# Loading one weight block in quarters and taking it up in turn: the first K projection of a gated mixer kernel

## The chip, the cores and the metric

The kernel runs on one core of a Trainium2 chip. The metric is device time in microseconds (us) of one execution, measured over several runs; the median counts. One further execution was recorded by the hardware profiler, and all lines shown as profile come from it. The engines are named as the profile does: PE is TensorE, DVE is VectorE, ACT is ScalarE, POOL is GpSimd and SP is SyncE, which here only issues DMAs.

## The reference

Two branches work on one input `x` of 2048 rows and 512 columns (bfloat16) and are mixed by a gate:

```python
x = A_x
g = _sigmoid((x * gate_w).sum(-1, keepdims=True))
a = _A_ref(x, A_wqkv, A_wo)
b = _B_ref(x, B_w1, B_b1, B_w2, B_b2)
return g * a + (1 - g) * b
```

Branch A is attention with 32 heads of 16 columns over a small window: each row looks at itself and at the seven rows that lie 2, 4, ... 14 rows before it. `x @ wqkv` gives Q, K and V; the logits are scaled by 0.25, rows before the start are masked, a softmax over the eight neighbours weights V, and the result goes through `wo`. Branch B is a LayerNorm of `x` over its columns, then a two-layer network across the rows: `w1` (2048 x 1792) with a bias and GELU, then `w2` (1792 x 2048) with a bias.

## The kernel before

**Tiling.** The rows of `x` are 16 tiles of 128 (`x0` to `x15`), and four blocks of 512 rows (`sb` 0 to 3) for the projections. Q, K and V are made transposed: one group is the output for one `dl` (0 to 3, a slice of 128 of the 512 columns) and one block `sb`. It sums over four slices of the input columns, so a group is four matmuls (L688) of 128x512 into one PSUM bank, followed by one evacuation on ScalarE (`evac`, recorded under the helper's line L469). The transposed `x` that they read comes for block 0 from TensorE transposes (`tx0` to `tx3`, L574, copied out by `ext0` to `ext3`) and for blocks 1 to 3 from DMA transposes (`xT1` to `xT3`, L496).

**Stages on TensorE.** Warm-up matmuls (L559), the transposes, and two short groups `lead0` and `lead1` (L605) of branch B; then the projections (48 groups, L688); then `ph2`, the first layer of branch B (L596), with `sum0` (L779), the logit sums of the first half of the rows, between its groups, and `sum1` for the second half; then `ph3`, the second layer (L913), with `wo0` to `wo15` (L922), the last projection of branch A, added to the same banks.

**Work beside it.** VectorE takes the LayerNorm statistics of each tile (`st2` to `st15`, L751) and some short steps from them (`ln_md` to `ln_mean`), the gate's sums (`z0` to `z15`, L732), the products of Q with shifted K (`qk`, L466), their sums (`qa`), the softmax, and the weighted sums of V (`avm`, `ava`, `avb`, `avc`). `qk0_0_512` is the product for the first half of the rows, `dl` 0, columns 512 on; `qk0_0_0` is that for the first 512. ScalarE evacuates the projections (`evq`, `evk`, `evv`), from block 2 on two groups at a time, and does logarithm, exponential and GELU; `ln_log` and `ln_rstd` are the two small steps that turn the variances into factors. GpSimd issues accumulating DMAs (`qd0`, `qd1_0`, `qd1_4`, `avd`) and gathers. SyncE issues the loads in a written order:

```python
ld_x(2, 2)
ld_w("wk01", 1, 0, 2, "wk")
ld_w("wk23", 1, 2, 4, "wk2")
...
ld_w("wq", 0, 0, 4, "wq")
ld_xt(1)
ld_x(4, 4)
ld_xt(2)
ld_x(8, 4)
ld_xt(3)
ld_x(12, 4)
ld_w("wv", 2, 0, 4, "wv")
```

`wk01` and `wk23` (L524, L525) hold the first and the last two of the four input slices of Wk, `x12` the tiles 12 to 15.

**What sets the order.** Every operation is added with a written duration, what it reads and what it writes. A list scheduler in the kernel (`_Sched`, L129 to L234) then fixes the order on each engine when the program is built. It takes at each step the operation that can start first in its own books; among those that can start at the same moment it takes the smallest value of minus the longest path to the end plus three times a written `prio`, so that a `prio` of -4 counts as 12 us of path (L196). The statistics have -4, the short LayerNorm steps -20. In its books a DMA moves 280 GB/s in a queue and lands 2 us after its last byte, and waiting for another engine adds 0.06. TensorE's operations are chained in the order in which they are written (`PE`, L565), except for `sum0` and `sum1`. On the chip each engine runs its list in that order, with semaphore waits.

**The place of the change.** For block 0 the kernel takes three K groups in halves, and then the rest:

```python
kb = [bank_() for _ in range(3)]
...
for tn, dl in ((0, 0), (0, 1), (0, 2), (1, 3), (0, 3)):
    proj(tn, dl, 0)
```

First come the first halves of three K groups, which need `wk01` alone, then their second halves (L702 and L704), each with its evacuation, and then whole groups: Q 0, Q 1, Q 2, K 3, Q 3. The banks for projections are taken in turn from four (4 to 7).

Of the kernel before, what the change touches and what calls it, by code (L numbers as in the profile page):

```python
# [317 lines left out]
def bass_gated_mix__sliding_local_dilated__mixer_token_mlp__prompt_kernel(nc, A_x, A_wqkv, A_wo, B_x, B_w1, B_b1, B_w2, B_b2, gate_w, out, dbg=None):  # L318
    with contextlib.ExitStack() as es:
# [64 lines left out]
        XTUSE = ["w1s3", "w1s4"]  # L384
# [67 lines left out]
        def col(v_, i):  # L452
            return bass.AP(v_.tensor, v_.offset + i, [list(v_.ap[0]), [1, 1]])
# [4 lines left out]
        def sub(ap_, offs, dims):  # L458
            return bass.AP(ap_.tensor, ap_.offset + offs, [list(ap_.ap[0])] + [list(d) for d in dims])
# [8 lines left out]
        def act(o_, i_, f_, **kw):  # L468
            return lambda e: e.activation(out=o_, in_=i_, func=f_, **kw)  # L469
# [21 lines left out]
        def load(name, dst, src, nbytes, writes, transpose=False, queue="sp", issue=0.5, order=True, deps=(), reads=()):  # L491
            ds = sch.dsem(name)

            def fn(e):
                if transpose:
                    return e.dma_start_transpose(dst, src)  # L496
                return e.dma_start(dst, src)  # L497
            op = sch.dma(queue, fn, nbytes, ds, issue=issue, reads=reads, writes=writes, deps=deps,
                         after=([last_ld[0]] if order and last_ld[0] is not None else []), name=name)
            if order:  # L500
                last_ld[0] = op
            return op

        def ld_x(t0, n):
            load("x%d" % t0, X[:, t0:t0 + n, :], xv[:, t0:t0 + n, :], n * 128 * D * 2, ["x%d" % t for t in range(t0, t0 + n)])

        def ld_w(name, tn, d0, d1, res):
            load(name, WQKV[:, d0:d1, tn * D:(tn + 1) * D], wqkv_v[:, d0:d1, tn * D:(tn + 1) * D], (d1 - d0) * 128 * D * 2, [res])
# [12 lines left out]
        ld_x(1, 1)  # L521
        ld_strip(0)
        ld_x(2, 2)
        ld_w("wk01", 1, 0, 2, "wk")  # L524
        ld_w("wk23", 1, 2, 4, "wk2")  # L525
        load("gw", GW1, bass.AP(gate_w.tensor, gate_w.offset, [[D, 1], [1, D]]), 1024, ["gwr"], issue=0.4, queue="act", order=False)
        load("b1", B1R, B_b1.rearrange("(t p) -> t p", p=128), 4096, ["b1r"], issue=0.4, queue="act", order=False)
        load("b2", B2R, B_b2.rearrange("(t p) -> t p", p=128), 4096, ["b2r"], issue=0.4, queue="act", order=False)
# [9 lines left out]
        def ld_w1(j):  # L538
            st = NLEAD if j < 2 else 0
            load("w1_%d" % j, W1S[W1AT[j]][:, st:NST, :], w1v[:, st:NST, 256 * j:256 * j + 256], (NST - st) * 128 * 256 * 2,  # L540
                 ["w1s%d" % W1AT[j]], order=j < 3)
# [23 lines left out]
        def PE(fn, dur, reads, writes, name, prio=0):  # L565
            op = A("pe", fn, dur, reads=reads, writes=writes, after=([chain[0]] if chain[0] is not None else []), name=name, prio=prio)
            chain[0] = op
            return op
# [23 lines left out]
        def f_ph2(ft, bank, s0, s1):  # L592
            def fn(e):
                ins = None
                for st in range(s0, s1):
                    ins = e.matmul(ps[:, bank, :], lhsT=W1S[W1AT[ft // 2]][:, st, 128 * (ft % 2):128 * (ft % 2) + 128], rhs=(LX if st < NLEAD else X)[:, st, :],  # L596
                                   start=(st == 0), stop=(st == NST - 1))
                return ins
            return fn
# [60 lines left out]
        def xt_res(sb):  # L660
            return XT0 if sb == 0 else ["xt%d" % sb]

        def evac(tn, dl, sb, bank):
            h, o = sb // 2, (sb % 2) * 512
            if tn == 0:
                dst = QH[h][:, dl, o:o + 512]
                A("act", act(dst, ps[:, bank, :], AF.Copy, scale=0.25), 0.6, reads=["b%d" % bank], writes=["q%d_%d" % (dl, sb)],
                  name="evq%d_%d" % (dl, sb))
            elif tn == 1:
                dst = KH[h][:, dl, PAD + o:PAD + o + 512]  # L670
                A("act", act(dst, ps[:, bank, :], AF.Copy), 0.6, reads=["b%d" % bank], writes=["k%d_%d" % (dl, sb)],
                  name="evk%d_%d" % (dl, sb))
            else:
                dst = V5[:, dl, PAD + sb * 512:PAD + (sb + 1) * 512]
                A("act", act(dst, ps[:, bank, :], AF.Copy), 0.6, reads=["b%d" % bank], writes=["v%d_%d" % (dl, sb)],
                  name="evv%d_%d" % (dl, sb))
        ring = [0, [4, 5, 6, 7]]

        def bank_():
            b = ring[1][ring[0] % len(ring[1])]  # L680
            ring[0] += 1
            return b

        def f_proj(tn, dl, sb, bank, d0=0, d1=4):
            def fn(e):
                ins = None
                for dt in range(d0, d1):
                    ins = e.matmul(ps[:, bank, :], lhsT=sub(WQKV, dt * 3 * D + tn * D + dl, [(4, 128)]),  # L688
                                   rhs=XT[:, dt, sb * 512:(sb + 1) * 512], start=(dt == 0), stop=(dt == 3))
                return ins  # L690
            return fn

        WR = {0: ["wq"], 1: ["wk", "wk2"], 2: ["wv"]}

        def proj(tn, dl, sb):
            bank = bank_()
            PE(f_proj(tn, dl, sb, bank), 0.87, xt_res(sb) + WR[tn] + XTUSE, ["b%d" % bank], "pj%s%d_%d" % ("qkv"[tn], dl, sb))
            evac(tn, dl, sb, bank)

        kb = [bank_() for _ in range(3)]  # L700
        for dl in range(3):
            PE(f_proj(1, dl, 0, kb[dl], 0, 2), 0.43, xt_res(0) + ["wk"], ["b%d" % kb[dl]], "pjk%d_0h" % dl)  # L702
        for dl in range(3):
            PE(f_proj(1, dl, 0, kb[dl], 2, 4), 0.43, xt_res(0) + WR[1] + XTUSE, ["b%d" % kb[dl]], "pjk%d_0" % dl)  # L704
            evac(1, dl, 0, kb[dl])
        for tn, dl in ((0, 0), (0, 1), (0, 2), (1, 3), (0, 3)):
            proj(tn, dl, 0)
        for dl in range(4):
            proj(1, dl, 1)
            proj(0, dl, 1)  # L710
# [1 line left out]
          reads=["k%d_1" % dl for dl in range(4)], writes=["khalo"], name="khalo")  # L712
        def proj2(tn, dl, sb):
            b0, b1 = bank_(), bank_()
            assert b1 == b0 + 1
            for b_, s_ in ((b0, sb), (b1, sb + 1)):
                PE(f_proj(tn, dl, s_, b_), 0.87, xt_res(s_) + WR[tn] + XTUSE, ["b%d" % b_], "pj%s%d_%d" % ("qkv"[tn], dl, s_))
            h = sb // 2
# [12 lines left out]
        for t in range(NST):  # L731
            A("dve", (lambda t_: lambda e: e.tensor_tensor_reduce(out=JUNK[:, t_ % 4, :], in0=X[:, t_, :], in1=GWB, scale=1.0, scalar=0.0, op0=ALU.mult, op1=ALU.add,  # L732
                                                                  accum_out=col(Z, t_)))(t), 0.61, reads=["x%d" % t, "gwb", "s4"], writes=["z%d" % t, "jk%d" % (t % 4)], after=[e3],
              name="z%d" % t, prio=-4)
        A("pool", lambda e: e.memset(ZN, 0.0), 0.15, writes=["zn"], name="zn0")
        A("dve", lambda e: e.tensor_scalar(out=ZN[:, 0:NST], in0=Z, scalar1=ZMAX, scalar2=-1.0, op0=ALU.min, op1=ALU.mult), 0.12,
          reads=["z%d" % t for t in range(NST)], writes=["zn"], name="zneg", prio=-30)
# [12 lines left out]
        for t in range(NLEAD, NST):  # L750
            A("dve", (lambda t_: lambda e: e.bn_stats(out=ST6[:, t_, :], in_=X[:, t_, :]))(t), 0.6,  # L751
              reads=["x%d" % t], writes=["st%d" % t], after=[e3], name="st%d" % t, prio=-4)
# [7 lines left out]
          reads=["md"], writes=["vv"], name="ln_var", prio=-20)  # L760
# [3 lines left out]
          reads=["ms", "rstd"], writes=["nmr"], name="ln_nmr", prio=-20)  # L764
        for t in range(NLEAD, NST):
            if t >= NST - LNACT:
                A("act", act(X[:, t, :], X[:, t, :], AF.Identity, scale=col(RSTD2, t), bias=col(NMR, t)), 0.7, after=[ev2[0][t - NST - 1]], reads=["rstd", "nmr"], writes=["x%d" % t],
                  name="ln%d" % t)
            else:
                A("dve", (lambda t_: lambda e: e.tensor_scalar(out=X[:, t_, :], in0=X[:, t_, :], scalar1=col(MS, t_), scalar2=col(RSTD2, t_),  # L770
                                                               op0=ALU.subtract, op1=ALU.mult))(t), 0.33,
                  reads=["rstd", "ms", "st%d" % t], writes=["x%d" % t], name="ln%d" % t, prio=-4)
# [14 lines left out]
        for h in range(2):  # L787
# [43 lines left out]
            if h == 0:  # L831
                A("dve", tt(psub(LOG[0], 0, 32, 0, [(UT_, NW), (1, PAD)]), psub(LOG[0], 0, 32, 0, [(UT_, NW), (1, PAD)]), MASK, ALU.add), 0.2,
                  reads=["mask"], writes=["log0"], name="msk")
# [16 lines left out]
            for c in range(4):  # L850
                for dhi in range(4):
# [5 lines left out]
                                   reads=["att%d" % h], writes=["avw%d_%d_%d" % (h, c, dhi)] + al, after=[prev] if prev else [],  # L857
                                   name="av%d_%d_%d" % (h, c, dhi))
# [10 lines left out]
        for u in range(8):  # L869
            h, c = u // 4, u % 4  # L870
            b = 1 if u % 2 == 0 else 0
# [3 lines left out]
              reads=["avw%d_%d_%d" % (h, c, dhi) for dhi in range(4)] + vr + ["vpad"], writes=PR[b], name="avm%d" % u)  # L875
# [15 lines left out]
        for ft in range(NFT):  # L891
            bank = ft if ft < GL else bank_()
            s0 = NLEAD if ft < GL else 0
            for a_, b_ in ((s0, 8), (8, NST)):
                PE(f_ph2(ft, bank, a_, b_), 0.2165 * (b_ - a_), ["%s%d" % ("lx" if t < NLEAD else "x", t) for t in range(a_, b_)] + ["w1s%d" % W1AT[ft // 2]],
                   ["b%d" % bank], "ph2_%d_%d" % (ft, a_))
            A("act", act(UT[:, ft, :], ps[:, bank, :], AF.Gelu_apprx_tanh, bias=col(B1C, ft)), 0.7, after=[xp0] if ft == 3 else [],
              reads=["b%d" % bank, "b1c"], writes=["ut%d" % ft] + (["wq", "wk", "wk2", "wv"] if ft == 0 else []), name="gel%d" % ft)
            if ft in (1, 3):
                ld_w1(5 + ft // 2)  # L900
        for j in range(8):
# [66 lines left out]
        for hf, (c0, c1) in enumerate(CH):  # L968
            bank = lastb[hf]
            n_ = c1 - c0  # L970
            PE(f_wo(L, bank, c0, c1), 0.87 * n_ / D, ["ot%d" % (L // 2), "wo"], ["b%d" % bank], "wo%d_%d" % (L, hf))
            if hf == 0:
                A("act", act(OUTS[:, NOUT, c0:c1], ps[:, bank, 0:n_], AF.Identity, scale=col(OMG, L), bias=col(C2, L)), 0.4,
                  reads=["b%d" % bank, "omg", "c2"], writes=["outl%d" % hf], name="ev%d_%d" % (L, c0))
# [80 lines left out]
```

## Time and profile before

| what | value |
|---|---|
| median of 3 runs | 164.26 us (164.2 to 165.22) |
| profiled execution, own time | 163.65 us |
| its span (first to last instruction) | 162.4 us |
| granted TensorE clock | 1.00 in the stretches looked at |
| busy: PE, DVE, ACT, POOL | 159.1, 150.7, 78.0, 26.7 us |
| PE waits for a load | 0.2 us, once, for a part of `wqkv` |

Busy times are sums over one engine; a busy PE is not a PE at its peak, since matmuls overlap and their ends are modelled. "L688 ... x12" means 12 instructions of line 688. What stands in brackets behind `<-` is what ended the idle time ahead of an instruction. Times are counted from the start of the span.

### The profile page before, as it was taken

The page shows a single profiled execution, that of the slowest core. Times are in us where ns is not written, and L with a number is a line of the kernel's source. Part 1 is how long each engine was busy: PE and PEld are TensorE (multiplying, and loading weights), DVE is VectorE, ACT ScalarE, POOL GpSimd, SP SyncE. Part 2 cuts the span into 40 slices and gives each one's busy share as a digit, 9 for nine tenths or more (in the row PEclk, how much of TensorE's full clock was granted, in tenths as well). Part 3 has the DMA queues.
Part 4 walks back from the last instruction along what each step waited for, and adds up shares of the span by engine and source line. Part 5 has one row for each costly group of instructions (what it writes and reads, how often), then busy time and mean ns, then how long its engine had stood idle before and what let it go on. Part 6 is the DMA issues. An engine that isn't in the chain of part 4 may idle for free.

```text
span 162.4 us, 1994 instructions
## 1 busy us (share of the span) xinstructions
PE 159.1 (98%) x779; PEld 75.9 (47%) x779; DVE 150.7 (93%) x140; ACT 78.0 (48%) x100; POOL 26.7 (16%) x62
## 2 busy tenths in 40 slices
PE   7999999999999999999999999999999999999994
PEld 2445555555554444444444344444444444444652
DVE  2879999999999999999899999999999999999943
ACT  4457665799998281999311345420121111111153
POOL 3000000300000011200792030009580003020000
DMA  5999999999925998999399999999999814949504
GB/s 136 282 218 244 249 312 291 290 262 241 196 63 166 297 290 156 169 292 188 93 292 356 338 295 256 240 322 290 352 215 216 195 39 95 184 110 199 128 32 162
DMA packets 45463, 35.54 MB, mean 219 GB/s; under 512 B 7949, under 2 KB 42254, under 8 KB 45454
## 3 DMA queue, kind: packets, MB, share of 16 engines
q1 hardware_dynamic: 41552, 22.74, 53.3%
q0 software_dynamic: 3696, 12.59, 36.2%
q8 instruction: 6, 0.10, 0.3%
q10 hardware_dynamic: 206, 0.08, 0.2%
q14 instruction: 3, 0.02, 0.0%
HBM read 19.15 MB, written 2.11 MB: 131 GB/s over the span
## 4 chain that ended last, share of the span: by engine, by line
PE 94%; DMA 3%; SPq 1%; DVE 0%; issue 0%
PE ps L913 30%; PE ps L596 29%; PE ps L688 26%; PE ps L922 9%; DMA arena<-in_A_wqkv_dram 3%; PE ps L779 1%; SPq L497 1%; DVE arena L931 0%
## 5 line engine op out<-in xcount | busy, mean ns | idle before, releaser
L466 DVE TENSOR_TENSOR arena<-arena 128x4096 bf16<-128x4096 bf16 (+6 forms) x71 | 125.9, 1806 | 2.7 <-ACT arena L469 1.1
L913 PE MATMUL ps<-arena 128*128 128x512 bf16 (+2 forms) x238 | 50.2, 366 | 0.0
L469 ACT ACTIVATE arena<-ps,arena 128x512 bf16<-128x512 f32 (+1 forms) x29 | 20.9, 727 | 57.1 <-PE ps L922 40.9
L596 PE MATMUL ps<-arena 128*128 128x512 bf16 x216 | 47.1, 379 | 0.0
L688 PE MATMUL ps<-arena 128*128 128x512 bf16 x192 | 41.8, 379 | 0.2 <-DMA arena<-in_A_wqkv_dram 0.2
L469 ACT ACTIVATE arena<-ps 128x512 bf16<-128x512 f32 (+3 forms) x37 | 31.2, 850 | 13.6 <-PE ps L688 9.1
L913 PEld LDWEIGHTS ps<-arena 128*128 128x128 bf16 x238 | 23.3, 98 | 25.4
L596 PEld LDWEIGHTS ps<-arena 128*128 128x128 bf16 x216 | 21.0, 98 | 25.8 <-issue 0.8
L688 PEld LDWEIGHTS ps<-arena 128*128 128x128 bf16 x192 | 21.6, 113 | 20.4 <-DVE arena L650 0.7
L856 POOL DMA_DIRECT2D arena<-arena x32 | 17.0, 660 | 23.1 <-DVE arena L466 14.0
L469 ACT ACTIVATE arena<-arena 128x512 bf16<-128x512 bf16 (+6 forms) x25 | 16.0, 641 | 9.5 <-DVE arena L466 8.9
L922 PE MATMUL ps<-arena 128*128 128x512 bf16 (+2 forms) x68 | 15.6, 366 | 0.0
L807 POOL DMA_DIRECT2D arena<-arena x3 | 3.8, 1270 | 63.0 <-DVE arena L466 35.9
L1004 ACT ACT_TABLE_LOAD x9 | 11.5, 1283 | 2.3 <-issue 2.2
L732 DVE CUSTOM_DVE_ANT_0 arena<-arena 128x512 bf16<-128x512 bf16 x16 | 10.1, 687 | 0.0
L877 POOL DMA_DIRECT2D arena<-arena x4 | 4.9, 1226 | 31.5 <-DVE arena L466 31.5
L922 PEld LDWEIGHTS ps<-arena 128*128 128x128 bf16 x68 | 6.6, 98 | 7.2
L751 DVE BATCH_NORM_STATS2 arena<-arena 128x6 f32<-128x512 bf16 x14 | 8.6, 679 | 0.0
L931 DVE TENSOR_SCALAR arena<-ps,arena 128x512 bf16<-128x512 f32 (+1 forms) x2 | 1.3, 660 | 3.4 <-PE ps L922 3.4
L610 DVE BATCH_NORM_STATS2 arena<-arena 128x6 f32<-128x512 bf16 x2 | 1.4, 678 | 3.0 <-DMA arena<-in_A_x_dram 3.0
L559 PE MATMUL ps<-const-bfloat16-1.0 128*128 128x512 bf16 x6 | 2.9, 580 | 0.8 <-PEq L1040 0.8
L779 PE MATMUL ps<-arena 128*32 128x512 bf16 x32 | 2.1, 382 | 0.0
(38 smaller groups left out, 16.8 us busy)
## 6 DMA issues: line engine op xcount, KB each, us to landing
arena<-in_B_w_dram SPq DMA_DIRECT2D x10, 896.0 KB, 11.6
arena<-arena POOLq DMA_DIRECT2D x6, 1024.0 KB, 9.5
arena<-in_B_w_dram SPq DMA_DIRECT2D x5, 1024.0 KB, 9.4
arena<-arena POOLq DMA_DIRECT2D x32, 128.0 KB, 7.5
arena<-arena POOLq DMA_DIRECT2D x1, 2048.0 KB, 16.3
out_dram<-arena SPq DMA_DIRECT2D x15, 128.0 KB, 1.8
arena<-in_A_x_dram SPq DMA_DIRECT2D x3, 512.0 KB, 4.7
arena<-in_A_wqkv_dram SPq DMA_DIRECT2D x2, 512.0 KB, 6.0
```

The lines of the kernel that those rows point to most:

```text
L466: return lambda e: e.tensor_tensor(out=o_, in0=a_, in1=b_, op=op_)
L469: return lambda e: e.activation(out=o_, in_=i_, func=f_, **kw)
L596: ins = e.matmul(ps[:, bank, :], lhsT=W1S[W1AT[ft // 2]][:, st, 128 * (ft % 2):128 * (ft % 2) + 128], rhs=(LX if st < NLEAD else X)[:, st, :],
L688: ins = e.matmul(ps[:, bank, :], lhsT=sub(WQKV, dt * 3 * D + tn * D + dl, [(4, 128)]), rhs=XT[:, dt, sb * 512:(sb + 1) * 512], start=(dt = ...
L732: A("dve", (lambda t_: lambda e: e.tensor_tensor_reduce(out=JUNK[:, t_ % 4, :], in0=X[:, t_, :], in1=GWB, scale=1.0, scalar=0.0, op0=ALU.m ...
L751: A("dve", (lambda t_: lambda e: e.bn_stats(out=ST6[:, t_, :], in_=X[:, t_, :]))(t), 0.6, reads=["x%d" % t], writes=["st%d" % t], after=[e ...
L807: qdl[0] = sch.dma("pool", (lambda d_, s_: lambda e: e.dma_start(d_, s_, accum_op=ALU.add, max_dma_last_dim=4096))(sub(PB[0], 4096 * b0, r ...
L856: prev = sch.dma("pool", (lambda d_, s_: lambda e: e.dma_start(d_, s_))(dst, src), 131072, ds, issue=1.0, reads=["att%d" % h], writes=["av ...
L877: sch.dma("pool", (lambda d_, s_: lambda e: e.dma_start(d_, s_, accum_op=ALU.add, max_dma_last_dim=4096))(sub(PB[b], 0, [(2048, 2), (1, 20 ...
L913: ins = e.matmul(ps[:, bank, 0:c1 - c0], lhsT=W2S[i // 2][:, ft, 128 * (i % 2):128 * (i % 2) + 128], rhs=UT[:, ft, c0:c1], start=(ft == 0) ...
L922: ins = e.matmul(ps[:, bank, 0:c1 - c0], lhsT=OT[:, i // 2, dl, 128 * (i % 2):128 * (i % 2) + 128], rhs=WO[:, dl, c0:c1], start=False, sto ...
L1004: e.preload_act_table_set(want)
```

## The change

The load of Wk is split into four loads, one for each input slice. For block 0 all four K groups now take a bank each; they take the first slice in turn, then the second in turn, and then each group takes its last two slices and is evacuated. The four Q groups follow. Each of these matmuls is now an operation of its own for the scheduler, with a written duration of 0.217. The names of the four loads take the place of the two wherever they are waited for or their place is written again.

```diff
-        ld_w("wk01", 1, 0, 2, "wk")
-        ld_w("wk23", 1, 2, 4, "wk2")
+        for d_ in range(4):
+            ld_w("wk%d" % d_, 1, d_, d_ + 1, "wk%d" % d_)
...
-        WR = {0: ["wq"], 1: ["wk", "wk2"], 2: ["wv"]}
+        WR = {0: ["wq"], 1: ["wk%d" % d_ for d_ in range(4)], 2: ["wv"]}
...
-        kb = [bank_() for _ in range(3)]
-        for dl in range(3):
-            PE(f_proj(1, dl, 0, kb[dl], 0, 2), 0.43, xt_res(0) + ["wk"], ["b%d" % kb[dl]], "pjk%d_0h" % dl)
-        for dl in range(3):
-            PE(f_proj(1, dl, 0, kb[dl], 2, 4), 0.43, xt_res(0) + WR[1] + XTUSE, ["b%d" % kb[dl]], "pjk%d_0" % dl)
+        kb = [bank_() for _ in range(4)]
+        for d_ in range(2):
+            for dl in range(4):
+                PE(f_proj(1, dl, 0, kb[dl], d_, d_ + 1), 0.217, xt_res(0) + ["wk%d" % d_], ["b%d" % kb[dl]], "pjk%d_0d%d" % (dl, d_))
+        for dl in range(4):
+            for d_ in (2, 3):
+                PE(f_proj(1, dl, 0, kb[dl], d_, d_ + 1), 0.217, xt_res(0) + ["wk%d" % d_] + (XTUSE if d_ == 3 else []), ["b%d" % kb[dl]], "pjk%d_0d%d" % (dl, d_))
             evac(1, dl, 0, kb[dl])
-        for tn, dl in ((0, 0), (0, 1), (0, 2), (1, 3), (0, 3)):
-            proj(tn, dl, 0)
+        for dl in range(4):
+            proj(0, dl, 0)
...
-              reads=["b%d" % bank, "b1c"], writes=["ut%d" % ft] + (["wq", "wk", "wk2", "wv"] if ft == 0 else []), name="gel%d" % ft)
+              reads=["b%d" % bank, "b1c"], writes=["ut%d" % ft] + (["wq", "wv"] + WR[1] if ft == 0 else []), name="gel%d" % ft)
```

## The prediction, made before the change was run

> **What bounds the kernel now.** I read the page first, then the chain of waits in order of time, then VectorE, ScalarE and SyncE in order of time around 20 to 30 us, then the landing times of single loads.
>
> ```profile
> span 162.4 us, 1994 instructions
> ...
> PE 159.1 (98%) x779; PEld 75.9 (47%) x779; DVE 150.7 (93%) x140; ACT 78.0 (48%) x100; POOL 26.7 (16%) x62
> ...
> PE 94%; DMA 3%; SPq 1%; DVE 0%; issue 0%
> ```
>
> TensorE is the bound, and VectorE stands close behind it. The chain, as start, length and what ran, shows how little the start can give:
>
> ```profile
> 2.72 4.59 DMA arena<-in_A_wqkv_dram
> 7.31 0.14 issue
> 7.45 2.75 PE ps L688 x12
> 10.20 0.01 issue
> 10.21 39.01 PE ps L688 x180
> 49.23 7.34 PE ps L596 x34
> 56.56 0.98 PE ps L779 x16
> ```
>
> 180 matmuls in 39.01 us are 0.2167 us each. The last matmul of lead1 (L605) starts at 6.84, so the next could start at 7.06; it starts at 7.45 because the first half of Wk lands at 7.31. The first 12 matmuls would take 2.60 at that pace and take 2.76 to the first Q matmul: 0.16 are spent waiting for Wq (issued at 3.74, 6.3 to landing, so 10.04). The most the start can give is 0.39 + 0.16 = 0.55 us, 0.3% of the time.
>
> VectorE, with its neighbours on ScalarE and SyncE:
>
> ```profile
> 20.48 0.68 DVE L751 BATCH_NORM_STATS2 arena<-arena 128x6 f32<-128x512 bf16 x1
> 21.07 2.27 DVE L466 TENSOR_TENSOR arena<-arena 128x4096 bf16<-128x4096 bf16 x1
> 23.32 2.47 DVE L751 BATCH_NORM_STATS2 arena<-arena 128x6 f32<-128x512 bf16 x4
> ...
> 26.26 0.17 DVE L759 SCALAR_TENSOR_TENSOR arena<-arena 128x16 f32<-128x16 f32 x1
> ...
> 26.65 2.29 DVE L466 TENSOR_TENSOR arena<-arena 128x4096 bf16<-128x4096 bf16 x1
> ```
>
> ```profile
> 25.09 1.02 ACT L469 ACTIVATE arena<-ps 128x1024 bf16<-128x1024 f32 x1 [0.70 <-PE ps L688]
> 26.46 0.47 ACT L469 ACTIVATE arena<-arena 128x16 f32<-128x16 f32 x2 [0.35 <-DVE arena L759]
> 26.84 1.00 ACT L469 ACTIVATE arena<-ps 128x1024 bf16<-128x1024 f32 x1
> ```
>
> ```profile
> 2.72 1.49 SPq L497 DMA_DIRECT2D arena<-in_A_wqkv_dram  x3
> 4.26 5.59 SPq L496 DMA_TRANSPOSE arena<-in_A_x_dram  x1
> ...
> 10.53 3.31 SPq L496 DMA_TRANSPOSE arena<-in_A_x_dram  x1
> ...
> 14.51 3.94 SPq L496 DMA_TRANSPOSE arena<-in_A_x_dram  x1
> 18.49 0.58 SPq L497 DMA_DIRECT2D arena<-in_A_x_dram  x1
> ```
>
> The last four row tiles of x (load x12) are issued at 18.49 and need 4.8 us to land: 23.29. VectorE starts their statistics (st12 to st15) at 23.32 without a wait, because the product qk0_0_512 (L791, 2.25 us from 21.07) stands ahead of them and fills just that time.
>
> **The change, part by part.** *Two loads become four.* SyncE's issues are 0.51 apart (2.72, 3.23, 3.74), so two more put Wq at 4.77, xT1 at 5.28 and all behind them up to 1.02 later. Whether landings move by that is not shown: between 0 and 1.02 for x12. I take the low end, 0.1. The three transposes of equal size held SyncE for 5.59, 3.31 and 3.94, so the first holds over 1.6 of waiting, which can swallow 1.02; and at 4.77 some 0.6 of the 1.3 MB up to Wk are still to move, so the DMA engines do not run dry. In half-microsecond windows xT1's small packets begin at 8 us, as Wq's large ones thin out: it waits for the queue and not for its issue. Against it speaks a slow stretch from 9 to 10 us, at 100 GB/s, where SyncE may be what is slow.
>
> A rule of the Trainium skill speaks against quarters: "DMA: Bandwidth & Descriptors", section "Bandwidth", asks for large transfers, and the section on the anatomy of a DMA gives about 2.0 us fixed for each, as completion latency. By that as an estimate, paid in turn, four quarters of 128 KB need 4 x 2.3 = 9.2 us, and K would start some 4.5 us later. The trace disagrees with paying it in turn: the halves, issued at 2.72 and 3.23, landed at 7.31 and 8.43, 1.1 apart.
>
> *The K groups.* Work is the same: 16 matmuls for K, then 16 for Q, instead of 12, 12, 4, 4. The first quarter lands before 7.31, so K may start between 7.06 and 7.45; gain 0 to 0.55, before anything downstream. q0 now stands behind 16 matmuls, and its evacuation behind four of K's (0.60 each, pitch 0.49 to 0.60). By rows: K at 7.06, q0's last matmul starts 19 x 0.2167 later at 11.18, ends 0.38 later, and evacuates at 11.6 to 12.2; at the latest 12.6. VectorE's first product, at 11.90 now after 1.09 idle, starts 0.3 to 0.7 later. That alone is covered: VectorE's sum sets TensorE's sum0 free at 55.61 (below), 0.95 ahead of its start at 56.56.
>
> *The order that the planner writes.* This is the part that costs. Orders are fixed at build time by the kernel's own list scheduler from its written durations (used here for the order alone, never as times). In its books K starts when lead1 ends, 8.068, in both kernels, since Wk lands earlier there. Before: q0 evacuates 11.648 to 12.248, qk0_0_0 and qk0_1_0 (2.2 each) end at 16.708, eight statistics of 0.6 end at 21.508; x12 is ready at 22.545, so qk0_0_512 goes first. After: K ends 16 x 0.217 later, four evacuations of 0.6 run 10.298 to 12.698, q0's to 13.298, the products start at 13.358 and end at 17.758, the eight statistics end at 22.558. Now x12 is ready, by 0.013. Both candidates can start; st12's key (128.55 of path plus its bonus of 12) beats qk0_0_512's 139.96, so st12 to st15 and the short LayerNorm steps go ahead of qk0_0_512. Likewise on ScalarE: ln_log is ready at 25.498 and the evacuation evk0_2 at 25.520, so ln_log and ln_rstd now stand ahead of evk0_2, which before went first.
>
> *What these orders cost on the chip.* VectorE waits with st12 until x12 lands: 23.29 + s (s, the load's delay, 0 to 1.02), so its statistics run as now, and qk0_0_512 comes afterwards: from 26.65 + s everything on VectorE is later by one product, 2.20 + s. ScalarE reaches ln_log at 26.46 + s, evk0_2 at 26.84 + s instead of 25.09, and ends it at 27.85 + s. Behind it waits TensorE: pjk1_2 takes the two banks that evk0_2 frees. At 0.2167 it is due 76 matmuls after 10.21, at 26.68; it starts at 27.9 + s. TensorE is 1.2 + s late, whatever it won at the start.
>
> The next meeting is sum0:
>
> ```profile
> 51.19 4.42 DVE L466 TENSOR_TENSOR arena<-arena 128x8192 bf16<-128x8192 bf16 x1
> ```
>
> It ends at 55.61; after, at 57.81 + s, and sum0 starts at 57.87 + s instead of 56.56: 1.3 + s late. TensorE arrives at 57.78 + s, so the two losses are one, not two. Behind sum0 TensorE's queue is matmuls only, so the delay is carried to the end. Later meetings: the second softmax (sum1) has slack, since qa1_2 ends at 89.92 and sum1 runs at 91.75; and at the end
>
> ```profile
> 155.32 0.69 DVE L466 TENSOR_TENSOR arena<-arena 128x1024 bf16<-128x1024 bf16 x1
> ```
>
> ends at 156.01, and wo12 needs it at 157.63: 1.6 slack, against VectorE's 2.2 to 2.5 less TensorE's 1.3. Also the planner then puts the first softmax ahead of two half products, so that the accumulating DMA qd1_4 is issued later (its DVE operand 3.7 later) and lands at about 81 instead of 78.7: VectorE has other work until about 80.7, so 0 to 0.4. All of that stays inside the slack; 0, up to 0.5 if not.
>
> **Sum.** 163.65 (the profiled execution: span 162.4 and 1.25 around it) + 1.3 + 0.1 = 165.05. The median of the runs shown is 0.61 above the profiled execution, so the median after should be 164.26 + 1.4 = 165.66, given as 165.7.
>
> **Rivals.** *The load's lag is carried through.* For it: SyncE issues without a pause from 0.81 to 20 us, and a longer list is simply later; s = 1.02 and 164.26 + 1.3 + 1.02 = 166.6. Against it: the transposes' unequal lengths.
>
> *The order does not tip.* The margins in the planner's books are 0.013 and 0.022 us, and a slip in my arithmetic would turn them. Then VectorE is 0.3 to 0.7 late, inside sum0's slack of 0.95, and TensorE keeps a gain of 0.2 to 0.55 at the start; VectorE then sets sum0 only from a gain of over 0.25 to 0.65 on. 164.26 - 0.3 = 164.0, not slower: the other side.
>
> *The quarters don't do what they say.* If wk0 lands no earlier than 7.31, the start stays, and only Wq's wait of 0.16 is covered by the fourth K group, as long as Wq lands before 10.9. With the order tipped this makes no difference, as pjk1_2's start does not depend on the start; without it 164.1.
>
> *VectorE becomes the bound to the end.* If qd1_4 or the gathered weights come late by over 0.7, wo12 waits: 0.5 more, 166.2.
>
> **How the numbers follow.** Tipped order with the load as now 0.52; tipped with the lag carried 0.24; VectorE's tail on top 0.08; not tipped (with the quarters that gain nothing) 0.16. About 1%, 1.64 us, is what a measurement of this kernel can tell from no change, and 1.4 is just under it: of the likeliest case I put 0.45 over the line, with the two worse cases 0.55 slower. Faster by over 1% has no mechanism, as the start holds 0.55 at most; 0.04 for orders that I did not foresee. Same is the rest, 0.41. The range runs from the untipped case, 164.0, to the carried lag with a little on top, 166.8; the likeliest case's own range is 165.3 to 166.2.
>
> **What would show it.** In the changed profile: VectorE idle for some 1.5 to 2 us before 23.3, released by the DMA of x; the product of 128x4096 from 21.07 now after 26.6; a TensorE gap of 1.2 to 1.7 us near 27.9 released by ScalarE's L469; sum0 at about 57.9 with next to no wait ahead of it; from there every start 1.3 to 1.4 later. The K start at 7.1 to 7.4 and no wait at the first Q would show the start's gain, lost again. The forecast is wrong if qk0_0_512 still runs at about 21.5, or if x12 lands at 24 or later.

## The result, and the profile after

The change made the kernel slower: 165.1 us median against 164.23, ratio 1.0058 with a 95% interval of 1.0037 to 1.0079; a repeat gave 1.0078 (1.0052 to 1.0103). The direction and the mechanism were those of the forecast; 165.7, a ratio of 1.0085 in the forecast's own working, was more than what came.

The page of the changed kernel, whose profiled execution took 165.7 us:

```profile
span 164.5 us, 1980 instructions
...
PE 159.4 (97%) x764; PEld 76.2 (46%) x779; DVE 150.5 (91%) x140; ACT 78.0 (47%) x100; POOL 26.7 (16%) x62
...
PE 81%; SPq 11%; DMA 3%; DVE 2%; issue 1%; ACT 1%
```

Busy times are those of before within 0.3 us, so no work was added. (PE shows x764 for 779 matmuls, since 15 of their records are missing from this trace; the weight loads, x779, are all there.) What changed is who sets the end: of the chain, TensorE holds 81% instead of 94%, and SyncE's queue 11%. The chain in order of time (start, length, what ran; the view leaves its shortest pieces out) says how, from SyncE to TensorE:

```profile
5.12 5.28 SPq L496
...
15.28 3.79 SPq L496
19.11 4.88 DMA arena<-in_A_x_dram
24.02 2.48 DVE arena L753 x4
27.41 1.14 ACT arena L469 x2
28.59 6.23 PE ps L688 x28
```

Before, the chain went from Wk's landing straight into matmuls. Now it goes through SyncE's list to the load x12 (issued at 19.11, landed at 23.99), the statistics st12 to st15, ScalarE's evacuation, and joins TensorE only at 28.59. VectorE and ScalarE around that place, in order of time:

```profile
17.82 4.84 DVE L753 BATCH_NORM_STATS2 arena<-arena 128x6 f32<-128x512 bf16 x8
24.02 2.47 DVE L753 BATCH_NORM_STATS2 arena<-arena 128x6 f32<-128x512 bf16 x4 [1.36 <-DMA arena<-in_A_x_dram]
...
27.34 2.29 DVE L466 TENSOR_TENSOR arena<-arena 128x4096 bf16<-128x4096 bf16 x1
...
29.63 2.29 DVE L466 TENSOR_TENSOR arena<-arena 128x4096 bf16<-128x4096 bf16 x1
```

```profile
24.00 1.02 ACT L469 ACTIVATE arena<-ps 128x1024 bf16<-128x1024 f32 x1 [1.13 <-PE ps L688]
27.16 0.46 ACT L469 ACTIVATE arena<-arena 128x16 f32<-128x16 f32 x2 [2.14 <-DVE arena L761]
27.53 1.92 ACT L469 ACTIVATE arena<-ps 128x1024 bf16<-128x1024 f32 x2
```

The product qk0_0_512, which stood at 21.07 ahead of the last four statistics, stands at 27.34 behind them; in its old place VectorE waits 1.36 for x12. On ScalarE the two small steps ln_log and ln_rstd hold up two evacuations, which ran at 25.09 and 26.84 before. TensorE pays, here in its waits (line, releaser, us in total, times, longest):

```profile
PE ps L688 <- ACT arena L469: 1.2, 1, 1.2
```

It is the only wait of TensorE for another engine or a load between its K start, at 8.26 here, and the end.

### The profile page after: what moved, and what is told of

It is laid out like the page before. It is cut to its first block, busy times and chain, and to the rows that moved or that the text cites. A ratio compares the mean times of both kernels' runs of the same rounds, so it can differ in the third digit from the quotient of the medians.

```text
span 164.5 us, 1980 instructions
## 1 busy us (share of the span) xinstructions
PE 159.4 (97%) x764; PEld 76.2 (46%) x779; DVE 150.5 (91%) x140; ACT 78.0 (47%) x100; POOL 26.7 (16%) x62
## 4 chain that ended last, share of the span: by engine, by line
PE 81%; SPq 11%; DMA 3%; DVE 2%; issue 1%; ACT 1%
PE ps L915 29%; PE ps L596 28%; PE ps L688 14%; PE ps L924 8%; SPq L496 8%; SPq L497 3%; DMA arena<-in_A_x_dram 3%; DVE arena L753 2%; PE ps L781 1%; ACT arena L469 1%; DVE arena L933 0%; DVE arena L466 0%; DVE arena L761 0%
## 5 line engine op out<-in xcount | busy, mean ns | idle before, releaser
L466 DVE TENSOR_TENSOR arena<-arena 128x4096 bf16<-128x4096 bf16 (+9 forms) x71 | 125.7, 1806 | 2.6 <-ACT arena L469 1.4
L596 PE MATMUL ps<-arena 128*128 128x512 bf16 x211 | 46.7, 379 | 0.4 <-issue 0.2
L688 PE MATMUL ps<-arena 128*128 128x512 bf16 x188 | 41.6, 379 | 1.4 <-ACT arena L469 1.2
L605 PE MATMUL ps<-arena 128*128 128x512 bf16 x8 | 2.8, 484 | 0.0
```

The lines of the kernel that those rows point to most:

```text
L466: return lambda e: e.tensor_tensor(out=o_, in0=a_, in1=b_, op=op_)
```

## The experiments

Two theories stood against each other. *Orders*: the four more K matmuls ahead of Q delay q0's evacuation in the scheduler's books, st12 to st15 pass qk0_0_512 by 0.013, and the waits that follow cost TensorE about 1 us. *Loads*: the quarters themselves, or SyncE's two more issues, cost it.

**The change with the old order.** One written duration is altered, no instruction:

```diff
-  PE(f_proj(1, dl, 0, kb[dl], d_, d_ + 1), 0.217, ...
+  PE(f_proj(1, dl, 0, kb[dl], d_, d_ + 1), 0.21, ...
```

> The change with one written duration altered: each K matmul counts 0.21 instead of 0.217 in the scheduler's books, so that qk0_0_512 goes ahead of st12 again and evk0_2 ahead of ln_log. The instructions are the same as in the change. Theory (the orders are what costs): no TensorE wait near 27.9, sum0 near 56.4 to 56.8, 0.3 less to 0.2 more than the kernel before (ratio 0.998 to 1.001). Rival (the four loads and SyncE's later issues are what costs): as the change, ratio 1.006.

Measured: ratio 0.9998 (0.9973 to 1.0023). TensorE's only wait in the profile is the usual one at launch. It runs through, in order of time:

```profile
8.99 41.60 PE L688 MATMUL ps<-arena 128*128 128x512 bf16 x192
50.43 7.50 PE L596 MATMUL ps<-arena 128*128 128x512 bf16 x34
57.86 1.05 PE L781 MATMUL ps<-arena 128*32 128x512 bf16 x16
```

Seven thousandths of a microsecond in the books of 16 operations, and the loss is gone, with quarters and four groups still there. (sum0 ran at 57.86 and not near 56.6, since K started late here, at 8.99. The order is not that of before in everything: ScalarE runs one more evacuation ahead of ln_log, and the change's later reordering, the first softmax ahead of two half products, is still in it; neither makes a loss that shows.)

**The old kernel with the new order.** The other way round, only the written size of one load differs:

```diff
-  ..., n * 128 * D * 2, ["x%d" % t ...
+  ..., n * 128 * D * 2 if t0 < 12 else 200000, ["x%d" % t ...
```

> The kernel before with nothing but the written size of the load x12 made smaller (200000 instead of 524288 bytes in the scheduler's books; the load itself is the same). That puts st12 to st15 ahead of qk0_0_512 and ln_log ahead of evk0_2, as in the change, and alters no other order; Wk in two loads, three K groups. Theory: x12 lands as before, pjk1_2 starts at 27.9 instead of 26.7 and sum0 at 57.9 instead of 56.6: 1.0 to 1.3 longer than before (ratio 1.006 to 1.008). Rival (loads): no difference, ratio 1.000.

Measured: ratio 1.0037 (1.0007 to 1.0066). TensorE and VectorE at the place:

```profile
29.51 22.64 PE L688 MATMUL ps<-arena 128*128 128x512 bf16 x104 [0.99 <-ACT arena L469]
```

```profile
24.93 2.47 DVE L751 BATCH_NORM_STATS2 arena<-arena 128x6 f32<-128x512 bf16 x4 [2.04 <-DMA arena<-in_A_x_dram]
```

TensorE waits 0.99 for ScalarE and starts pjk1_2 at 29.51, not 27.9; VectorE waits 2.04 for x12, which landed late in this execution (24.9). So the tip alone makes a loss, with two loads and three groups. Its size came below the 1.006 to 1.008 expected, and its interval is wide enough for less than the change's loss or all of it.

**The loads alone.** The quarters, and nothing else:

```diff
-  ld_w("wk01", 1, 0, 2, "wk")
-  ld_w("wk23", 1, 2, 4, "wk2")
+  for d_ in range(4):
+      ld_w("wk%d" % d_, 1, d_, d_ + 1, "wk%d" % d_)
```

> The kernel before with Wk loaded in four quarters and nothing else: three K groups take both first quarters at once, as before. The orders on VectorE and ScalarE are those of before. Theory: two more issues on SyncE move x12's landing by 0.6 to 1.0, which st12 waits for, inside VectorE's slack of 0.95 before sum0: ratio 0.999 to 1.001. Rival (loads): 1.004 or more.

Measured: ratio 0.9999 (0.9976 to 1.0023), which leaves the rival's 1.004 out. Loads are not the cause.

**Taking the quarters in turn, with the old order of groups.**

```diff
-  kb = [bank_() for _ in range(4)]
+  kb = [bank_() for _ in range(3)]
...
-  for dl in range(4):
-      proj(0, dl, 0)
+  for tn, dl in ((0, 0), (0, 1), (0, 2), (1, 3), (0, 3)):
+      proj(tn, dl, 0)
```

The two loops over K groups run to 3 as well.

> Quarters, and the three K groups of before take the first two quarters in turn; then the groups follow in the order of before (Q 0, Q 1, Q 2, K 3, Q 3). The orders on VectorE and ScalarE are those of before. Theory: TensorE starts K 0 to 0.4 earlier and waits for Wq up to 0.7 more, so that at most 0.3 is left: ratio 0.998 to 1.000. Rival (loads): 1.004 or more.

Measured: ratio 0.9996 (0.997 to 1.0021). Taking up the first quarter alone brings nothing that can be measured; why, is told below.

**ScalarE's order put back.** The change, with ln_log behind evk0_2:

```diff
+  byn = {op.name: op for op in sch.ops}
+  byn["ln_log"].order.add(byn["evk0_2"])
   est = sch.schedule()
```

> The change with one order put back: ln_log stands behind evk0_2 on ScalarE, as before; VectorE keeps the change's order. Theory (two meetings, TensorE's pjk1_2 with ScalarE and its sum0 with VectorE, that fall on the same delay): the wait near 28 goes, and one of 1.0 to 1.3 appears ahead of sum0; the time stays that of the change, ratio 1.005 to 1.006. Rival (ScalarE's order alone costs): ratio 1.000.

Measured: ratio 1.0046 (1.0016 to 1.0077). TensorE in order of time in that kernel:

```profile
7.92 41.77 PE L688 MATMUL ps<-arena 128*128 128x512 bf16 x192
...
58.19 1.05 PE L781 MATMUL ps<-arena 128*32 128x512 bf16 x16 [1.15 <-DVE arena L466]
```

The wait near 28 is gone, and one of 1.15 stands ahead of sum0, released by VectorE. The two meetings are one loss, as VectorE's lateness reaches sum0 anyway: mending one of them brings nothing.

**No wait for x12.** The change, with the statistics of tiles 12 to 15 taken from tiles 8 to 11:

```diff
-  in_=X[:, t_, :]
+  in_=X[:, t_ - 4 if t_ > 11 else t_, :]
...
-  reads=["x%d" % t]
+  reads=["x%d" % (t - 4 if t > 11 else t)]
```

> The change, but st12 to st15 take their statistics from tiles 8 to 11, which are there, and so do not wait for the load x12 (the statistics of tiles 12 to 15 are left out). All orders are those of the change. Theory (the price is the wait for x12): VectorE idles nowhere near 23, TensorE does not wait near 28 nor at sum0, and the span is the K start plus 154.8, as in the kernels with the old order: ratio 0.998 to 1.001. Rival (the order as such): as the change, 1.005 or more.

Measured: ratio 1.0004 (0.998 to 1.0028). VectorE, in order of time, now runs twelve statistics in a row, and TensorE waits nowhere near 28:

```profile
17.18 7.23 DVE L753 BATCH_NORM_STATS2 arena<-arena 128x6 f32<-128x512 bf16 x12
...
25.28 2.29 DVE L466 TENSOR_TENSOR arena<-arena 128x4096 bf16<-128x4096 bf16 x1
```

So the order as such costs nothing; what costs is that in this order VectorE idles for x12. The expected span was missed: K start 7.62 and 154.8 make 162.4, and it was 163.3, since TensorE, early in this execution, waited 0.71 for the transposed x (xT3) and went on at 23.17.

**x12 ahead of xT3.** The change with two issues swapped:

```diff
-  ld_xt(3)
-  ld_x(12, 4)
+  ld_x(12, 4)
+  ld_xt(3)
```

> The change with the load x12 issued ahead of the transposing load xT3 instead of behind it; the orders on VectorE, ScalarE and TensorE are those of the change. Theory (what costs is VectorE's wait for x12, not the order as such): x12 lands near 20, VectorE does not wait, TensorE does not wait near 28; xT3 lands near 23, about when TensorE needs it: ratio 0.998 to 1.002. Rival (the order as such costs, by the product that it puts off): 1.005 or more.

Measured: ratio 1.013 (1.0075 to 1.0186), and both theories missed. TensorE in that kernel:

```profile
24.70 5.52 PE L688 MATMUL ps<-arena 128*128 128x512 bf16 x17 [2.78 <-DMA arena<-in_A_x_dram]
```

The wait near 28 went, but xT3 is now late, and TensorE waits 2.78 for it. That is not the whole loss: the 17 matmuls of this line take 5.52, where 0.2167 each would make 3.7. The granted clock reads 0.50 from 25 to 28 us in this profile and 1.00 again from 29 on, so TensorE came out of the wait slow and lost some 1.6 more. (After the shorter waits of 0.71 to 1.67 in the other profiles it stayed at 1.00.) As a test of the wait for x12 it is inconclusive, since one late load took the place of another; the run before settled that. It shows that xT3 can't be put off by one load without TensorE waiting for it.

**Delaying the K start.** Four idle matmuls ahead of the first K group, in both kernels:

```diff
+  PE(f_warm(4, 4), 0.001, [], ["b4"], "warm3")
   kb = [bank_() for _ in range(3)]      # range(4) in the change
```

> The kernel before with four idle matmuls of 128x512 ahead of the first K group, written as 0.001 in the scheduler's books, so that no order changes. Theory (before, TensorE is bound from its K start to the end): the four, 0.87 at 0.2167 each, show in full: ratio 1.005. Rival (the end is not set by the K start): 1.000 to 1.002.

> The change with the same four idle matmuls ahead of its first K matmul, the orders being those of the change. Theory (the change's time hangs on the landing of x12, and not on the K start; TensorE waited 1.18 near 28): the 0.87 are taken out of that wait: ratio to the kernel before 1.006 to 1.007, as the change without them. Rival (the change's loss sits elsewhere and adds): 1.011.

Measured: 1.0118 (1.0071 to 1.0164) for the old kernel, and 1.0065 (1.0033 to 1.0096) for the change. The ratio of the change stays at that without the idle work, as expected if the wait takes it up. Its profile does not show the wait shrink: x12 landed late there too (st12 at 24.61), K started at 8.26 as in the first profile, and the wait is 1.67. In the old kernel it shows, and more than the 0.87 expected: 1.9 us by the median of six runs. The profiled execution has just 0.87 (leads end near 7.82, K at 8.69, span 163.5). Four matmuls at the slow rate of 0.427 would be 1.7, which would fit; that the timed executions ran them at that rate is not shown.

**Both kernels again.**

> The kernel before, unchanged. Theory: ratio 1.000; the span is the K start plus 154.8, and the K start is later than the 7.45 of its first profile in most executions (near 8 to 9), since the two lead groups run at 0.427 a matmul until TensorE speeds up. Rival (7.45 is usual for it): K at 7.4 to 7.5.

> The change, unchanged. Theory: ratio 1.006; the span is the start of st12 plus 140.5, whatever the K start is, with one wait of TensorE near 28. Rival: the span follows the K start.

Measured: 1.002 (0.9991 to 1.0049) for the same kernel against itself, which shows what such a comparison can tell, and 1.0078 for the change. The spans were 162.9 with a K start of 8.01, and 164.6 with st12 at 24.16 (154.9 and 140.4 apart). TensorE again waits once near 28, 1.33.

## Why the prediction was right, and where its size was off

**What sets the end.** Over eleven of the thirteen profiles one line holds for each order (left out are the two runs that change where x12 is needed or loaded; there TensorE waits for xT3 instead):

| order on VectorE | kernel | starts at | span | difference |
|---|---|---|---|---|
| old: K start | before | 7.45 | 162.4 | 154.95 |
| | quarters alone | 7.96 | 162.8 | 154.8 |
| | before again | 8.01 | 162.9 | 154.9 |
| | late start, before | 8.69 | 163.5 | 154.8 |
| | change, cost 0.21 | 8.99 | 163.8 | 154.8 |
| | three groups in turn | 9.19 | 164.0 | 154.8 |
| new: start of st12 | ScalarE's order back | 23.64 | 164.1 | 140.5 |
| | change | 24.02 | 164.5 | 140.5 |
| | change again | 24.16 | 164.6 | 140.4 |
| | late start, change | 24.61 | 165.1 | 140.5 |
| | tip alone | 24.93 | 165.4 | 140.5 |

With the old order the K start sets the end; with the new one, the landing of x12 does, whatever the K start is (7.88 to 9.37 in those five).

**The orders.** All that was worked out by hand came true: st12 to st15 ahead of qk0_0_512, ln_log ahead of evk0_2, the first softmax ahead of two half products, sum1 one half group later. So did the two meetings: pjk1_2 follows x12's landing by 4.6 (23.99 to 28.59), as the sum had it (23.29 to 27.9), and qa0_2 ends at 58.50 just ahead of sum0 at 58.56.

**The load's delay.** It was taken as 0.1. The profile of the change shows 0.70 more than that of before, but this is the spread of executions: the issue of x12 lies at 18.23 to 20.03 in four profiles with halves (mean 18.96) and at 18.57 to 19.53 in eight with quarters (mean 19.04). The means differ by 0.1; with this spread in so few profiles a shift of some tenths more or less can't be told from it, but the full 1.02 does not show. The reason given fits: the first transpose holds SyncE for 5.79 on average with halves and 4.97 with quarters, so that waiting took up some 0.8 of the 1.02. Wk's quarters landed at 6.4, 7.1, 7.9 and 9.0 in the profile of the change, so no fixed cost was paid in turn. (The section that the prediction cites for 2.0 us is on DMAs issued by GpSimd, and these loads are SyncE's. Nor would paying it in turn hold K back to the fourth quarter, since K starts on the first.)

**The step that failed** is that from 165.05 to 165.66: "The median of the runs shown is 0.61 above the profiled execution, so the median after should be 164.26 + 1.4". The 1.3 in it was worked out against a K start at 7.45, and that execution was an early one. The old kernel's median of 164.23 is a span of 163.0, with the 1.25 around it, and so a K start near 8.1 by the table; in the three later comparisons the median of its spans on record is 163.0 to 163.2, against 162.4 in the profile. But with the new order the end hangs on x12 and not on the K start, as the prediction itself says of pjk1_2. The 0.6 to 0.7 by which a usual execution starts later are time that TensorE would have spent waiting; they lessen the loss, and the step added them to the end. Without it the sum is 165.05, and 165.1 was measured; for that x12 has to land in the median execution about as early as in the profile before, which no profile shows. What the runs showed in place of 1.4 is a loss of 0.95 by the ratio 1.0058, and of 1.3 by the repeat. That the profiled execution of the change took just 165.7 is luck: x12 landed 0.70 later in it than in the profile before.

The measured 165.1 lies just under the 165.3 to 166.2 given for the likeliest case, and the loss of over 1%, to which the forecast gave 0.55, did not come. Of the signs named, the places came true and the times only about: VectorE idled 1.36 instead of 1.5 to 2, sum0 ran at 58.56 instead of 57.9, K at 8.26 instead of 7.1 to 7.4. One sign of being wrong, x12 at 24 or later, was missed by 0.01 in the first profile and met in the repeat (24.1), though the mechanism was there: the limit was drawn from one profile, and x12's issue varies by more than a microsecond.

For the same reason the start could not give its 0.55: in the other profiles with the old order Wk is there before TensorE is through with its lead groups. Where these ran as early as in the first profile, in the run with x12 ahead of xT3, K started at 7.08 with the quarters instead of 7.45, so that 0.37 of the gain is there in such an execution. The lead groups differ like this, first those of the old kernel, then those of three groups in turn:

```profile
4.88 1.04 PE L605 MATMUL ps<-arena 128*128 128x512 bf16 x4
...
6.20 1.03 PE L605 MATMUL ps<-arena 128*128 128x512 bf16 x4
```

```profile
5.19 1.86 PE L605 MATMUL ps<-arena 128*128 128x512 bf16 x4
...
7.70 1.65 PE L605 MATMUL ps<-arena 128*128 128x512 bf16 x4
```

Four matmuls take 1.04 at full rate (three steps of 0.2167 and 0.38 for the last) and 1.86 at half rate (three of 0.427 and about 0.6). In this execution TensorE sped up only in the second lead group, and K started at 9.19. (In the repeat of the old kernel, with K at 8.01, the first lead group waited 0.8 for VectorE instead.) The Trainium skill has this in "TensorE: Matmul & The Clock Gate", Part 1: the clock goes up after a busy window that runs freely, so that the number of slow matmuls varies from run to run of one kernel. The traces agree: in the two profiles of the change, one kernel, the first lead group takes 1.74 and 1.02. Over all profiles K starts from 7.08 to 9.37, part of it by other waits ahead of it.

**The rivals.** The lag carried through, 166.6, did not come. The untipped order is what the run with 0.21 made of the change, and it showed no gain: 0.9998, where that rival came to 0.998, which the interval (0.9973 to 1.0023) does not rule out. VectorE's tail stayed inside its slack: its last evacuation still waited 3.2 for TensorE at the end.

**What stays open.** The profiled execution of the change took 0.6 more than its median, those of the old kernel 0.6 and 0.4 less than theirs; no profile shows st12 before 23.64, where the median of 165.1 asks for 23.4. Where x12 lands in the timed runs is not on record, so that the account of the size rests on their spans.

No version tried here shows a gain over the old kernel.

## What to carry to other kernels

Where a list scheduler writes the orders, work out what an edit does to its ties before costing the edit: here a gain of at most 0.55 at the start bought a reordering some 15 us later that cost 0.9 to 1.3, and 0.007 in a written duration took it back. Before a sum is made from one profiled execution, ask whether its start is typical; here the K start, behind matmuls at the slow clock, moved by up to 2.3, more than such a change is worth. An order that lets an engine wait for a load is cheap in the scheduler's books when the load lands there 0.013 earlier than the engine is free, and dear on the chip when it does not.

## What the runs showed of the hardware that was not expected

The column of the granted clock reads 1.00 in the first ten microseconds of every profile that was looked at, also where matmuls of 128x512 step at 0.427 instead of 0.2167; the slow start shows only in the instructions. After TensorE's wait of 2.78 in the run with x12 ahead of xT3 the same column does show it, 0.50 from 25 to 28 us, and the matmuls there again step at about 0.43. And a transposing load holds its issuing engine for long, it seems until what is queued ahead of it has moved: the first of three equal ones held SyncE for 4.48 to 6.62 us, the second for 3.3 to 3.7, and the third for 5.65 where two plain loads stood ahead of it, against 3.56 to 4.23 behind one. Two more issues ahead of the first moved x12's issue by 0.1 on average, within the spread.
